# One decode block on Trainium2: a new order in TensorE's attention loop, and w_down's odd rows loaded another way

## The chip, the core and the metric

The kernel runs on one core of a Trainium2 chip. The metric is the device time of one execution in microseconds (us); its median over 15 runs is compared. A profile of one execution stands beside the times. The engines are called PE (TensorE's matmuls), PEld (TensorE's weight loads), DVE (VectorE), ACT (ScalarE), POOL (GpSimd) and SP (SyncE, which here only issues DMAs). L181 is line 181 of the kernel.

## What is computed

One token goes through an attention block with a cached K and V, and then through a gated feed-forward block. There are 32 heads of 128, 4096 cached positions, a model width of 640 and a feed-forward width of 1728. All inputs are bf16.

```python
def _A_ref(x, k_cache, v_cache, wq, wo):          # x: layernorm of the token
    q = (x @ wq).reshape(B, Sq, 32, 128).transpose(0, 2, 1, 3)
    scores = jnp.einsum("bhqd,bhkd->bhqk", q, k_cache) * (128 ** -0.5)
    o = jnp.einsum("bhqk,bhkd->bhqd", softmax(scores), v_cache)
    return o.transpose(0, 2, 1, 3).reshape(B, Sq, 4096) @ wo
def _B_ref(x, w_gate, w_up, w_down):
    return (gelu(x @ w_gate) * (x @ w_up)) @ w_down
x = A_x
h = x + _A_ref(layernorm(x), A_k_cache, A_v_cache, A_wq, A_wo)
h2 = h + _B_ref(layernorm(h), B_w_gate, B_w_up, B_w_down)
```

K and V are 32 MB each, so the kernel reads 84.2 MB for one token.

## The kernel before

**Stages.** The 32 heads are taken in eight stages (`NG`) of four heads. A stage's K is one DMA of 4 MB into one of two slots (`k_slot`), its V one DMA of 4 MB into the single `v_slot`; the last V goes into `k_slot[0]`. Partition 32h + p of a slot holds 128 consecutive positions of head h.

**Work of a stage G.** DVE multiplies K by the query in two halves, `mult(G, 0)` and `mult(G, 1)` (L368), into `prod`. TensorE adds up groups of the products with the identity matrix, `fold(e, 0)` and `fold(e, 1)`: 16 matmuls each into PSUM banks 0 to 3 (L349, and L181 for those that keep the weights). `probs(G)` then has DVE reduce the four banks to the scores (L374), ACT take the exponential (L375), and POOL multiply the result by the head mask `own` into `p_bd` (L377, called the mask multiply here). `pv` is 32 matmuls of `p_bd` with V into bank 5 (L356); ACT copies that bank out (L382), and `head_sum` (L362) picks the heads' parts.

**The order.** A small program builder (`Prog`) keeps a list of operations for each engine; each engine runs its list in order, and waits are written from the dependencies. TensorE's list has a hardware loop over k = 1 to 7, whose body is fold 0 of stage k, PV of stage k-1, fold 1 of stage k, head sum of stage k-1. The fold waits for its multiply and for the previous reduce. DVE's list has mult(1,0), the reduce of stage 0 and mult(1,1) at its start, and from then on both multiplies of a stage and then its reduce.

**SP's queue.** It issues W_q, K0, K1, V0, and then K2, V1, K3, V2 and so on to V7. A K load waits for the second multiply of the stage two before it; V(g) waits for PV(g-1). Behind them come W_o in two halves, w_down's odd rows, w_gate and w_up (both into `v_slot`, after PV 6), and the rest of w_down in four loads. w_down's 1728 rows are taken as three blocks of 512 (four rows to a partition) and 192 odd rows, the first of the matrix: 64 partitions with three rows each, in eight loads of eight partitions (L437 to L439), which wait for the last K multiply.

**The tail.** After PV 7 come the sums of the softmax, the output projection in two halves (L451), the residual and the second layernorm, the gate and up products (`glu`, L476, 75 matmuls each), the gelu on DVE and ACT (L483 to L491), and the down product (L494 to L506), whose first matmuls take the odd rows with 64 partitions. `pad_program` (L165) puts 200 instructions at the end of TensorE's program that are jumped over.

The constants come from POOL and DVE at the start: DVE clears bank 5 (L292) and builds `of_i` and `hs` from the identity matrices (L297, L298).

Of the kernel before, what the change touches and what calls it, by code (L numbers as in the profile page):

```python
# [5 lines left out]
FP32 = mybir.dt.float32  # L6
BF16 = mybir.dt.bfloat16
ALU = mybir.AluOpType
ACTF = mybir.ActivationFunctionType
AX = mybir.AxisListType  # L10

D = 640
# [8 lines left out]
NG = 8  # L21
# [140 lines left out]
                    inst.then_inc(lp.ev[ks[0], lp.body[n][0]].sem, 1)  # L162


def pad_program(nc, e, n):  # L165

    on = [e.engine]
    never = nc.alloc_registers("never", engines=on)
    nc.regs_mov(never, 0)
    nc.br_eq(nc.snap(never, min_val=0, max_val=1), 1, on_true="spare", on_false="done", engines=on)  # L170
    here = nc.cur_bb
    nc.switch_bb("spare")
    for i in range(n):
        e.nop(hint="n", nofuse=True)
    nc.br("done", engines=on)
    nc.switch_bb("done", parent=here)


def held(e, out, lhsT, rhs, start, stop):

    built = e.matmul(out, lhsT, rhs, start=start, stop=stop)  # L181
# [13 lines left out]
def bass_sequential_preLN__gqa_block_cached__glu_gated_geglu__decode_kernel(nc, A_x, A_k_cache, A_v_cache, A_wq, A_wo, B_x, B_w_gate, B_w_up, B_w_down, out):  # L195
    sb = lambda name, shape, dt: nc.alloc_sbuf_tensor(name, shape, dt)
# [5 lines left out]
    qb = sb("qb", [128, NG, DH], BF16)  # L202
    sc = sb("sc", [128, 128], FP32)
    pt = sb("pt", [128, 128], BF16)
    own = sb("own", [128, 4], BF16)
    p_bd = sb("p_bd", [128, 128, 4], BF16)
    RS = sb("RS", [128, NG], FP32)
# [8 lines left out]
    hlnT = sb("hlnT", [128, 5], BF16)  # L216
    po_sb = sb("po_sb", [128, 512], FP32)
    hs = sb("hs", [128, 4, 4], FP32)
# [3 lines left out]
    of_i = sb("of_i", [128, 32], BF16)  # L222
    g_t = sb("g_t", [128, 15], FP32)
# [6 lines left out]
    ones_f = sb("ones_f", [128, 128], FP32)  # L230
    mean_f = sb("mean_f", [128, 128], FP32)
    ones_b = sb("ones_b", [128, 128], BF16)
    id_f = sb("id_f", [128, 128], FP32)
    id_b = sb("id_b", [128, 128], BF16)
    eps_t = sb("eps_t", [128, 1], FP32)
# [3 lines left out]
    ps_f = psum[:, 0:2048]  # L239
    ps_q = [bank[0], bank[1]]  # L240
    ps_g, ps_u, ps_p = bank[0], bank[1], bank[2]
    ps_a = bank[4]
    ps_d = bank[3]
    ps_o = bank[5]
# [7 lines left out]
    P = Prog(nc)  # L252
    V = lambda fn, *d: P.op("vector", fn, *d)
    A = lambda fn, *d: P.op("scalar", fn, *d)
    T = lambda fn, *d: P.op("tensor", fn, *d)
    GP = lambda fn, *d: P.op("gpsimd", fn, *d)
# [9 lines left out]
    mults, pvs = {}, {}  # L266
# [10 lines left out]
    for kind, g in order[:3]:  # L277
# [8 lines left out]
    c_idb = GP(lambda e: e.affine_select(id_b[:, :], ones_b[:, :], pattern=[[1, 128]], compare_op=ALU.is_equal,  # L286
                                         fill=0.0, base=0, channel_multiplier=-1), c_onesb)
    c_ones = GP(lambda e: e.memset(ones_f[:, :], 1.0))
    c_idf = GP(lambda e: e.affine_select(id_f[:, :], ones_f[:, :], pattern=[[1, 128]], compare_op=ALU.is_equal,
                                         fill=0.0, base=0, channel_multiplier=-1), c_ones)  # L290

    c_po = V(lambda e: e.memset(ps_o, 0.0))  # L292
    own0 = GP(lambda e: e.affine_select(own[:, :], ones_b[:, 0:4], pattern=[[-32, 4]], compare_op=ALU.is_ge,
                                        fill=0.0, base=0, channel_multiplier=1), c_onesb)
    c_own = GP(lambda e: e.affine_select(own[:, :], own[:, :], pattern=[[32, 4]], compare_op=ALU.is_ge,
                                         fill=0.0, base=31, channel_multiplier=-1), own0)
    c_of = V(lambda e: e.tensor_reduce(of_i[:, :], id_b[:, :].rearrange("p (q i) -> p i q", q=4), axis=AX.X, op=ALU.max), c_idb)  # L297
    c_hs = V(lambda e: e.reduce_sum(hs[:, :, :], id_f[:, :].rearrange("p (t x r j) -> p x r j t", t=4, x=2, r=4)[:, 0, :, :, :],  # L298
                                    axis=AX.X), c_idf)


    def x_cols(e):
# [36 lines left out]

    reds, exps, blocks, evs, folds = {}, {}, {}, {}, {}  # L340
    VM = lambda fn, *d: P.op("vector", fn, *d, chan="m")
    VR = lambda fn, *d: P.op("vector", fn, *d, chan="r")
    AS = lambda fn, *d: P.op("scalar", fn, *d, chan="s")
    GS = lambda fn, *d: P.op("gpsimd", fn, *d, chan="s")

    def fold(e, i):
        for b in range(16):
            s, n = divmod(b, 8)
            mm = held if b else lambda e, *a, **k: e.matmul(*a, **k)  # L349
            r = mm(e, bank[2 * i + s], id_b[:, :], prod[:, i, 32 * s:32 * s + 32, 16 * n:16 * n + 16], start=(n == 0), stop=(n == 7))  # L350
        return r
# [14 lines left out]
    def mult(G, i):  # L366
        kt = view(k_slot[G % 2])
        mults[G, i] = VM(lambda e: e.tensor_tensor(  # L368
            out=prod[:, i, :, :], in0=kt[:, 64 * i:64 * i + 64, :],
            in1=qb[:, G, :].unsqueeze(1).to_broadcast([128, 64, DH]), op=ALU.mult),  # L370
            landed["K"][G], qa, qc, folds.get((G - 1, i)))

    def probs(G):
        reds[G] = VR(lambda e: e.reduce_sum(sc[:, :], ps_f.rearrange("p (g d) -> p g d", d=16), axis=AX.X), folds[G, 1])  # L374
        exps[G] = AS(lambda e: e.activation(pt[:, :], sc[:, :], ACTF.Exp, bias=zero_t[:, 0:1],  # L375
                                            scale=INV_SQRT_DH, accum_out=RS[:, G:G + 1]), reds[G], c_eps)
        blocks[G] = GS(lambda e: e.tensor_tensor(  # L377
            out=p_bd[:, :, :], in0=pt[:, :].unsqueeze(2).to_broadcast([128, 128, 4]),
            in1=own[:, :].unsqueeze(1).to_broadcast([128, 128, 4]), op=ALU.mult), exps[G], c_own)

    def evacuate(G):
        evs[G] = AS(lambda e: e.copy(po_sb[:, :], ps_o), pvs[G])  # L382

    def body_fold(i):
        return ("f%d" % i, lambda e, k: fold(e, i), lambda k: [mults[k, i], reds[k - 1]], True)

    for i in range(2):
        mult(0, i)
        folds[0, i] = T(lambda e, i=i: fold(e, i), mults[0, i], c_idb, qa, qc)
    T(None, c_hs, c_po)  # L390
    lp = P.loop("tensor", range(1, NG), [
        body_fold(0),
        ("pv", lambda e, k: pv(e, view(v_slot)), lambda k: [blocks[k - 1], landed["V"][k - 1]], True),
        body_fold(1),
        ("h", lambda e, k: head_sum(e, k * 4 - 4), lambda k: [evs[k - 1]], False)])
    for k in range(1, NG):
        for i in range(2):
# [1 line left out]
        pvs[k - 1] = lp.ev[k, "pv"]  # L399
    for kind, g in order[3:5]:  # L400
        load(kind, g)
    mult(1, 0)
    probs(0)
    mult(1, 1)
    for G in range(1, NG):
        if G > 1:
            mult(G, 0)
            mult(G, 1)
        for kind, g in order[3 + 2 * G:5 + 2 * G]:
            load(kind, g)  # L410
        evacuate(G - 1)
        probs(G)

    rt = GP(lambda e: e.tensor_tensor(out=RT[:, :, :], in0=RS[:, :].unsqueeze(2).to_broadcast([128, NG, 4]),
                                     in1=own[:, :].unsqueeze(1).to_broadcast([128, NG, 4]), op=ALU.mult), exps[NG - 1])
    pvs[NG - 1] = T(lambda e: pv(e, view(v_of(NG - 1))), blocks[NG - 1], landed["V"][NG - 1])
    T(lambda e: e.matmul(ps_z[:, 0:H], ones_f[:, :], RT[:, :, :].rearrange("p g j -> p (g j)"),
                         start=True, stop=True), rt, c_ones)
# [3 lines left out]
    at = V(lambda e: e.tensor_tensor(out=aT[:, :], in0=ps_a[:, 0:H], in1=RT[:, :, :].rearrange("p g j -> p (g j)"), op=ALU.mult), zr)  # L422
    as_ = V(lambda e: e.tensor_tensor(out=aS[:, :, :], in0=aT[:, :].unsqueeze(2).to_broadcast([128, H, 4]),
                                      in1=own[:, :].unsqueeze(1).to_broadcast([128, H, 4]), op=ALU.mult), at)
# [9 lines left out]
    wd_sb = k_slot[1][:, 0:15 * D].rearrange("p (m n) -> p m n", m=15)  # L434
    wd_v = B_w_down[192:1728, :].rearrange("(a p r) n -> p a r n", a=3, r=4)
    wd_d = wd_sb[:, 0:12, :].rearrange("p (a r) n -> p a r n", a=3)
    for o in (0, 1, 2, 3, 32, 33, 34, 35):  # L437
        d_wp = P.dma("sync", wd_sb[o:o + 29:4, 12:15, :],
                     B_w_down[0:192, :].rearrange("(p r) n -> p r n", r=3)[o:o + 29:4, :, :], mults[NG - 1, 1], chan="wp")  # L439
    d_wg = P.dma("sync", wg_sb, B_w_gate[:, :].rearrange("(p c) n -> p c n", c=5), pvs[NG - 2])  # L440
    d_wu = P.dma("sync", wu_sb, B_w_up[:, :].rearrange("(p c) n -> p c n", c=5))
    d_wd = [P.dma("sync", wd_d[:, a, lo:hi, :], wd_v[:, a, lo:hi, :])
# [28 lines left out]
    def glu(ps, w, *ws):  # L471
        def fn(e):
            for c in range(5):
                for m in range(15):
                    at, step = (192 + 512 * (m // 4) + m % 4, 4) if m < 12 else (m - 12, 3)
                    i = e.matmul(ps[:, m:m + 1], w[:, c, at:at + 127 * step + 1:step], hlnT[:, c:c + 1],  # L476
                                 start=(c == 0 and m == 0), stop=(c == 4), skip_group_check=True)
            return i
        return T(fn, *ws)
    ga = glu(ps_g, wg_sb, hl, d_wg)  # L480

    up = glu(ps_u, wu_sb, d_wu)
    g1 = V(lambda e: e.tensor_copy(g_t[:, :], ps_g[:, 0:15]), ga)  # L483
    g2 = V(lambda e: e.tensor_mul(t1[:, :], g_t[:, :], g_t[:, :]), g1)
    g3 = V(lambda e: e.scalar_tensor_tensor(out=t2[:, :], in0=t1[:, :], scalar=1.0 / GELU_C1, in1=g_t[:, :],
                                            op0=ALU.add, op1=ALU.mult), g2)
# [6 lines left out]
    def down(ms, qs=range(4)):  # L493
        def fn(e):  # L494
            for m in ms:
                for q in qs:
                    rows = 128 if m < 12 else 64
                    i = e.matmul(ps_d[32 * q:32 * q + 1, 0:160], hm[0:rows, m:m + 1],  # L498
                                 wd_sb[0:rows, m, 160 * q:160 * q + 160], start=False, stop=(m == 11))
            return i  # L500
        return fn
    T(down(range(12, 15)), g9, d_wp)
    T(down(range(4)), d_wd[0])
    T(down(range(4, 8)), d_wd[1])
    T(down(range(8, 11)), d_wd[2])
# [6 lines left out]
    P.op("sync", None, d_out)  # L512

    P.emit({"sync": 2})
    pad_program(nc, nc.tensor, 200)


# [26 lines left out]
```

## Time and profile before

| | us |
|---|---|
| median of 15 runs | 203.1 (202.2 to 204.7) |
| the profiled execution | 203.25 |
| its span, first to last instruction | 201.9 |
| busy: PE, DVE, POOL, ACT | 119.8, 98.8, 25.1, 12.6 |
| DMA: bytes moved, mean rate | 84.32 MB, 418 GB/s |

The profiled execution's time is 1.35 us longer than its span, which runs from the first to the last instruction of the program. The median is 0.15 us below that execution. In the profile's rows a group is given by line, engine, operation and tiles (written tile first, then what was read), with the number of instructions; in the timeline the columns are the start, the length, the group, and in brackets the idle time of the engine before it and what ended it. "Landing" is the moment at which a DMA's completion is counted; a load over all 128 partitions is spread over 16 DMA engines, and each of them counts its own completion.

### The profile page before, as it was taken

Reading aid. Unit: us, or ns where it says so; the run is one execution under the profiler, and the core shown is the slowest. Engines: PE = TensorE matmul, PEld = TensorE weight load, DVE = VectorE, ACT = ScalarE, POOL = GpSimd, SP = SyncE. Lnnn points to the kernel's source line nnn. Section 1 sums busy time; section 2 is a strip of 40 time slices with the busy share of each in tenths; the row PEclk is TensorE's granted clock in tenths of the full one; section 3 lists DMA queues with packets and bytes.
Section 4 is the critical chain, followed back from the end, with each engine's and each line's share of the span. In section 5 each row is a group of like instructions: output and inputs, shape, how many; then the busy total and the mean of one; then the engine's idle time right before and its main releaser. Section 6 shows DMA issues by size and latency. Waiting matters only on the chain.

```text
span 201.9 us, 1983 instructions
## 1 busy us (share of the span) xinstructions
PE 119.8 (59%) x1008; PEld 31.6 (16%) x748; DVE 98.8 (49%) x52; ACT 12.6 (6%) x33; POOL 25.1 (12%) x23
## 2 busy tenths in 40 slices
PE   0107029759908943990598069808940993976655
PEld 0101000001200120120012001200120012476543
DVE  2201196992299169627922791399149804020321
ACT  2101000000100100010001000100100010100101
POOL 3000000044062008002000200072010002000000
PEclk9999555967985995896579757975995599665555
DMA  9999999999999999999999999999999999999991
GB/s 357 414 404 461 428 422 422 422 467 441 419 422 415 415 428 467 448 422 415 415 422 474 441 428 415 415 422 474 428 435 422 415 422 441 410 427 434 423 387 58
DMA packets 3738, 84.32 MB, mean 418 GB/s; under 512 B 467, under 2 KB 597, under 8 KB 1045
## 3 DMA queue, kind: packets, MB, share of 16 engines
q1 hardware_dynamic: 3730, 84.23, 97.4%
q8 instruction: 5, 0.08, 0.2%
q10 hardware_dynamic: 2, 0.00, 0.0%
q14 instruction: 1, 0.00, 0.0%
HBM read 84.23 MB, written 0.00 MB: 417 GB/s over the span
## 4 chain that ended last, share of the span: by engine, by line
DMA 52%; PE 25%; DVE 19%; SPq 3%; issue 1%; DVEq 0%
DMA k_slot<-in_A_k_cache_dram 38%; PE psum L181 17%; DVE prod L368 15%; DMA v_slot<-in_B_w_up_dram 14%; PE psum L356 4%; DVE sc L374 3%; SPq L59 3%; PE psum L349 2%; PE psum L476 1%; PE psum L498 1%; DVE out_row L507 0%; DVE hm L491 0%; DVEq L114 0%
## 5 line engine op out<-in xcount | busy, mean ns | idle before, releaser
L368 DVE TENSOR_TENSOR prod<-k_slot,qb 128x8192 bf16<-128x8192 bf16 x16 | 73.2, 4608 | 12.1 <-DMA k_slot<-in_A_k_cache_dram 9.9
L181 PE MATMUL psum<-prod,id_b 128*128 128x512 bf16 x240 | 72.0, 467 | 0.0
L374 DVE TENSOR_REDUCE sc<-psum 128x128 f32<-128x2048 f32 x8 | 18.3, 2290 | 47.2 <-PE psum L181 47.2
L377 POOL TENSOR_TENSOR p_bd<-pt,own 128x512 bf16<-128x512 bf16 x8 | 23.1, 2892 | 145.5 <-ACT pt L375 145.5
L349 PE MATMUL psum<-prod,id_b 128*128 128x512 bf16 x16 | 7.9, 496 | 55.0 <-DVE prod L368 51.6
L356 PE MATMUL psum<-v_slot,p_bd 128*16 128x512 bf16 x224 | 13.3, 379 | 0.0
L349 PEld LDWEIGHTS psum<-prod,id_b 128*128 128x128 bf16 x16 | 1.6, 100 | 68.8 <-DVE prod L368 52.8
L356 PEld LDWEIGHTS psum<-v_slot,p_bd 128*16 128x16 bf16 x224 | 5.0, 89 | 45.3 <-DMA v_slot<-in_A_v_cache_dram 22.2
L362 PEld LDWEIGHTS psum<-hs,po_sb 128*128 128x128 f32 x64 | 8.3, 191 | 22.8 <-issue 22.1
L382 ACT COPY po_sb<-psum 128x512 f32<-128x512 f32 x7 | 4.1, 586 | 83.1 <-PE psum L356 83.1
L362 PE MATMUL psum<-hs,po_sb 128*128 128x4 f32 x64 | 7.7, 244 | 0.4 <-ACT po_sb L419 0.4
L451 PE MATMUL psum<-aP,arena 128*128 128x1 bf16 x160 | 6.7, 178 | 1.9 <-DMA arena<-in_A_wo_dram 1.8
L375 ACT ACTIVATE pt<-sc,zero_t 128x128 bf16<-128x128 f32 x8 | 3.2, 402 | 60.0 <-DVE sc L374 60.0
L331 PE MATMUL psum<-arena,xlnB 128*32 128x512 bf16 x20 | 2.8, 530 | 7.0 <-DMA arena<-in_A_wq_dram 7.0
L451 PEld LDWEIGHTS psum<-aP,arena 128*128 128x128 bf16 x160 | 6.6, 131 | 2.1 <-DMA arena<-in_A_wo_dram 1.9
L476 PE MATMUL psum<-hlnT,v_slot 128*128 128x1 bf16 x150 | 5.1, 171 | 2.5 <-DMA v_slot<-in_B_w_up_dram 2.5
L476 PEld LDWEIGHTS psum<-hlnT,v_slot 128*128 128x128 bf16 x150 | 5.0, 115 | 3.1 <-DMA v_slot<-in_B_w_up_dram 2.6
L356 PE MATMUL psum<-k_slot,p_bd 128*16 128x512 bf16 x32 | 3.4, 602 | 3.2 <-POOL p_bd L377 3.2
L336 DVE CAST qb<-psum 128x512 bf16<-128x512 f32 x1 | 0.7, 692 | 9.1 <-PE psum L181 9.1
L457 DVE COPY hT<-psum 128x5 f32<-128x5 f32 x1 | 0.2, 165 | 8.6 <-PE psum L451 8.6
L304 PE MATMUL psum<-one_bf,x_row 1*128 1x1 bf16 x5 | 0.4, 177 | 6.7 <-DMA x_row<-in_A_x_dram 6.7
L421 DVE RECIPROCAL RT<-psum 128x32 f32<-128x32 f32 x1 | 0.4, 357 | 6.9 <-PE psum L362 6.9
(63 smaller groups left out, 28.3 us busy)
## 6 DMA issues: line engine op xcount, KB each, us to landing
k_slot<-in_A_k_cache_dram SPq DMA_DIRECT2D x8, 4096.0 KB, 24.8
v_slot<-in_A_v_cache_dram SPq DMA_DIRECT2D x7, 4096.0 KB, 16.6
arena<-in_A_wq_dram SPq DMA_DIRECT2D x1, 5120.0 KB, 15.0
arena<-in_A_wo_dram SPq DMA_DIRECT2D x2, 2560.0 KB, 35.1
k_slot<-in_A_v_cache_dram SPq DMA_DIRECT2D x1, 4096.0 KB, 26.6
v_slot<-in_B_w_gate_dram SPq DMA_DIRECT2D x1, 2160.0 KB, 23.5
v_slot<-in_B_w_up_dram SPq DMA_DIRECT2D x1, 2160.0 KB, 28.2
k_slot<-in_B_w_down_dram SPq DMA_DIRECT2D x2, 640.0 KB, 30.1
```

Source lines behind the costliest of these rows:

```text
L59: ev = self.op(eng, lambda e: e.dma_start(out, in_), *deps, dma=True, chan=chan)
L181: built = e.matmul(out, lhsT, rhs, start=start, stop=stop)
L349: mm = held if b else lambda e, *a, **k: e.matmul(*a, **k)
L356: i = e.matmul(ps_o[a:a + 16, :], p_bd[:, 4 * b:4 * b + 4, :].rearrange("p g j -> p (g j)"), vt[:, 4 * b:4 * b + 4, :], start=(b < 4), sto ...
L362: i = e.matmul(ps_a[:, bass.ds(at, 4)], po_sb[:, 128 * r:128 * r + 128], hs[:, r, :], start=(r == 0), stop=(r == 3))
L368: mults[G, i] = VM(lambda e: e.tensor_tensor(out=prod[:, i, :, :], in0=kt[:, 64 * i:64 * i + 64, :], in1=qb[:, G, :].unsqueeze(1).to_broad ...
L374: reds[G] = VR(lambda e: e.reduce_sum(sc[:, :], ps_f.rearrange("p (g d) -> p g d", d=16), axis=AX.X), folds[G, 1])
L375: exps[G] = AS(lambda e: e.activation(pt[:, :], sc[:, :], ACTF.Exp, bias=zero_t[:, 0:1], scale=INV_SQRT_DH, accum_out=RS[:, G:G + 1]), red ...
L377: blocks[G] = GS(lambda e: e.tensor_tensor(out=p_bd[:, :, :], in0=pt[:, :].unsqueeze(2).to_broadcast([128, 128, 4]), in1=own[:, :].unsquee ...
L382: evs[G] = AS(lambda e: e.copy(po_sb[:, :], ps_o), pvs[G])
L451: r = e.matmul(ps_p[:, c:c + 1], wo_sb[:, i, c::5], aP[:, i:i + 1], start=False, stop=(i == 31), skip_group_check=True)
L476: i = e.matmul(ps[:, m:m + 1], w[:, c, at:at + 127 * step + 1:step], hlnT[:, c:c + 1], start=(c == 0 and m == 0), stop=(c == 4), skip_grou ...
```

## The change

The body of TensorE's loop becomes PV of stage k-1, fold 0, fold 1, head sum. The fold no longer waits for the reduce by itself, since PV, which now stands ahead of it, waits for what follows the reduce. Stage 0's reduce stands on DVE before both multiplies of stage 1. The mask multiply of stages 0 and 7 moves from POOL to DVE; for stage 0 a one-element memset on POOL passes the signal on.

w_down's 192 odd rows become one load of 128 rows, one to a partition, and eight loads of four partitions with two rows each into a new tile `wd_lo`, which POOL clears at the start. In `wd_lo` rows 0 to 15 and 32 to 47 hold data. The gate and up products take the matching columns with step 1 instead of 3, and the gate's copy becomes a multiply by `own_g`, which is zero in the partitions that hold no row. The down product takes 128 partitions once and 48 twice, instead of 64 three times.

Bank 5 is cleared by a matmul with zero weights (`none_b`) before the loop, and `hs` and `of_i` are made by four selects each on POOL. `pad_program` goes.

```diff
-def pad_program(nc, e, n):
...
-    c_po = V(lambda e: e.memset(ps_o, 0.0))
...
-    c_of = V(lambda e: e.tensor_reduce(of_i[:, :], ...
-    c_hs = V(lambda e: e.reduce_sum(hs[:, :, :], ...
+    c_hs = c_own
+    for t in range(4):
+        c_hs = GP(lambda e, at=at: e.affine_select(hs[at, :, :], ...
+    c_of = c_hs
+    for t in range(4):
+        c_of = GP(lambda e, at=at: e.affine_select(of_i[at, :], ...
+    c_none = GP(lambda e: e.memset(none_b[:, :], 0.0), c_of)
+    GP(lambda e: e.memset(own_g[:, 0:13], 1.0))
...
+    c_wd = GP(lambda e: e.memset(wd_lo[:, :, :], 0.0), c_gm)
...
+        on = V if G in (0, NG - 1) else GS
+        blocks[G] = on(lambda e: e.tensor_tensor(
             out=p_bd[:, :, :], in0=pt[:, :].unsqueeze(2).to_broadcast([128, 128, 4]),
             in1=own[:, :].unsqueeze(1).to_broadcast([128, 128, 4]), op=ALU.mult), exps[G], c_own)
+        if G == 0:
+            blocks[G] = GS(lambda e: e.memset(spare[:, :], 0.0), blocks[G])
...
-        return ("f%d" % i, lambda e, k: fold(e, i), lambda k: [mults[k, i], reds[k - 1]], True)
+        return ("f%d" % i, lambda e, k: fold(e, i), lambda k: [mults[k, i]], True)
...
-    T(None, c_hs, c_po)
+    T(lambda e: e.matmul(ps_o, none_b[:, :], qb[:, 0:4, :].rearrange("p g d -> p (g d)"), start=True, stop=True), c_none)
+    T(None, c_hs)
     lp = P.loop("tensor", range(1, NG), [
-        body_fold(0),
         ("pv", lambda e, k: pv(e, view(v_slot)), lambda k: [blocks[k - 1], landed["V"][k - 1]], True),
-        body_fold(1),
+        body_fold(0), body_fold(1),
         ("h", lambda e, k: head_sum(e, k * 4 - 4), lambda k: [evs[k - 1]], False)])
...
-    mult(1, 0)
     probs(0)
-    mult(1, 1)
     for G in range(1, NG):
-        if G > 1:
-            mult(G, 0)
-            mult(G, 1)
+        mult(G, 0)
+        mult(G, 1)
...
+    d_w1 = P.dma("sync", wd_sb[:, 12, :], B_w_down[64:192, :], mults[NG - 1, 1])
     for o in (0, 1, 2, 3, 32, 33, 34, 35):
-        d_wp = P.dma("sync", wd_sb[o:o + 29:4, 12:15, :],
-                     B_w_down[0:192, :].rearrange("(p r) n -> p r n", r=3)[o:o + 29:4, :, :], mults[NG - 1, 1], chan="wp")
+        lo = o - o % 32
+        d_wp = P.dma("sync", wd_lo[o:o + 13:4, :, :],
+                     B_w_down[lo:lo + 32, :].rearrange("(r i q) n -> q i r n", q=4, r=2)[o - lo, :, :, :], c_wd, chan="wp")
...
-    g1 = V(lambda e: e.tensor_copy(g_t[:, :], ps_g[:, 0:15]), ga)
+    g1 = V(lambda e: e.tensor_tensor(out=g_t[:, :], in0=ps_g[:, 0:15], in1=own_g[:, :], op=ALU.mult), ga, c_gm)
...
-                    rows = 128 if m < 12 else 64
+                    rows, wd = (128, wd_sb[:, m]) if m < 13 else (48, wd_lo[:, m - 13])
...
-    T(down(range(12, 15)), g9, d_wp)
+    T(down([12]), g9, d_w1)
+    T(down([13, 14]), d_wp)
...
-    pad_program(nc, nc.tensor, 200)
```

## The prediction

> **What bounds the kernel now.** I read the page's slices first, because they say whether any engine matters at all.
>
> ```profile
> span 201.9 us, 1983 instructions
> ...
> DMA  9999999999999999999999999999999999999991
> ...
> q1 hardware_dynamic: 3730, 84.23, 97.4%
> q8 instruction: 5, 0.08, 0.2%
> ```
>
> The 16 DMA engines are full from the first slice to the last but one. The change moves the same bytes, so it can only act on holes in that stream, on how evenly its tail falls on the 16 engines, and on work behind the last landings. The chain that ended last, in order of time, shows the tail:
>
> ```profile
> 166.57 28.21 DMA v_slot<-in_B_w_up_dram
> 194.78 0.05 issue
> 194.83 2.58 PE psum L476 x75
> ...
> 197.73 2.35 PE psum L498 x51
> 200.08 0.30 DVE out_row L507
> ```
>
> w_up lands at 194.78, its product takes 2.58, the down product 2.35. In the trace's landing records the last w_down load completes on its sixteenth engine at 199.70, and the last four matmuls start at 199.74: two chains end within 0.4 us of each other. The same records show an uneven stream. From 64 us on, two engines complete every K and V load about 1.0 us after the third-last (V6: 160.46, then 161.46, 161.52). A 16 KB packet of the instruction queue (52.66, 183.72, 193.14, each 1.0 us) sits on one DMA engine, and the data packet behind it is 0.35 to 0.55 us longer: some 1.5 us for each. The last load's completions are 196.91 to 198.40 on fourteen engines, then 199.47 and 199.70.
>
> Last, the timeline of the last attention stage, where the new order acts:
>
> ```profile
> 156.70 5.57 PE L181 MATMUL psum<-prod,id_b 128*128 128x512 bf16 x15
> 162.21 1.90 PE L356 MATMUL psum<-v_slot,p_bd 128*16 128x512 bf16 x32
> 164.04 0.39 PE L349 MATMUL psum<-prod,id_b 128*128 128x512 bf16 x1
> 164.27 3.40 PE L181 MATMUL psum<-prod,id_b 128*128 128x512 bf16 x15
> 167.71 2.29 DVE L374 TENSOR_REDUCE sc<-psum 128x128 f32<-128x2048 f32 x1 [7.13 <-PE psum L181]
> 170.03 0.40 ACT L375 ACTIVATE pt<-sc,zero_t 128x128 bf16<-128x128 f32 x1 [5.28 <-DVE sc L374]
> 170.60 1.04 POOL L377 TENSOR_TENSOR p_bd<-pt,own 128x512 bf16<-128x512 bf16 x1 [18.90 <-ACT pt L375]
> 171.69 3.39 PE L356 MATMUL psum<-k_slot,p_bd 128*16 128x512 bf16 x32 [3.24 <-POOL p_bd L377]
> ```
>
> Fold 0 runs from 156.30 to 162.21 while V6 is still landing (161.52). PV, fold 1, reduce, exp, mask and the last PV follow.
>
> **PV first in the loop.** V(k-1) lands one load after K(k), so fold 0 of every stage, which needed only K(k), now stands on TensorE behind a PV that waits for V(k-1) and for the mask; behind fold 0 wait fold 1, DVE's reduce, ACT's copy and SP's next V load. The work after that landing becomes PV 1.83 (162.21 to 164.04) and two folds at full clock, 3.63 each (164.04 to 167.67): 9.09. To this comes the cold start. Granted clock is 0.5 when a stage begins, and fold 0 shows its price: 5.30 to 6.48 us over the seven stages, against 3.63 for fold 1, so 1.67 to 2.85, mean 2.25. Today that is paid before V lands; now it is paid after. Fold 1 then ends at 161.57 + 9.09 + 2.25 = 172.9 instead of 167.67: 5.2 later (4.7 to 5.8).
>
> [...]
>
> Most stages have cover. DVE has to reduce (2.29) and then multiply the next K (two of 4.8, beside POOL) after fold 1, which ends 23.4 us after V(k-1) landed; V(k) lands after 19.4, and its PV and fold 0 cover the other 4.0. V(k+1)'s load is issued when PV(k) ends, 1.9 us after V(k) landed today and about 3.4 then; K(k+2) still has over 6 us to run. So the stream keeps its next load and the steady stages cost nothing; without that cover each would cost the excess.
>
> In the last stage the shift goes on. The reduce and exp keep their durations. The mask goes to DVE, which is idle there. VectorE multiplies with the same broadcast took 0.29 for 128 elements and 0.82 for 640 f32; POOL took 1.04. I take 0.67 for 512 (0.165 for five elements, plus four times 0.127), so 0.4 saved (0.2 to 0.75). The last PV took 3.32 because the clock had fallen at 171.33, 2.9 us after the loop's last matmul; then it starts 2.8 us after it. Half a warm PV is worth 0.75 (0 to 1.5). PV ends 5.2 - 0.4 - 0.75 = 4.05 later, and so does the first half of the output projection: 185.7 instead of 181.66. The second half waited for W_o until 183.49, so it starts 2.25 late, and the gate product ends at 192.36 + 2.25 = 194.6. w_up lands at 194.78. The cover is used up but for 0.2, and the bounds give -1.2 to +1.3 around it: on average I charge 0.25.
>
> **The 192 odd rows of w_down.** 64 packets of 3840 B at 149 ns (9.5 us of engine time) become 192 of 1280 B at 55 ns (10.6): 0.07 per engine if spread evenly. It is not even. Chaining packets end to start, today's 64 sit on eight engines, eight packets each (1.2 us), and the two late engines carry none. The new 128-partition load gives every engine eight packets: 0.44, also the late ones. The 64 rows left, 3.5 us of engine time, add between 0.22 (all engines) and 0.88 (four engines). On the late engine that ends last I take 0.45 (0.44 to 1.32): last landing 200.15. On the eight, the fast engine hit at 183.72, which sets w_up's landing, goes from 1.2 to between 0.44 and 1.32: -0.8 to +0.1.
>
> [...]
>
> SP's queue: the first small load waits for the last K multiply, 160.58 now and about 165.5 then. Nine issues at 0.66 and the six large ones (2.8) are behind it, done by 174.3; the DMA engines reach them at 181.4. Cover 7 us, cost zero.
>
> **Edits with one answer.** The eight selects and the memsets on POOL run at the start: the present set ends at 3.0, and even a 2.1 us memset for wd_lo ends by 8.5; TensorE needs them at 39. The DVE work they replace lies before x lands at 6.7. The zeroing matmul (0.39) stands at 39.0, when TensorE is idle until 42.4. In stage 0 the reduce and the mask stand on DVE before both multiplies of K1; the mask waits some 0.6 for ACT's exp, and those multiplies wait behind it: the second ends at 51.5 instead of 46.7. K3's load waits for it, but V1's, issued before, is 10 us long. The mask's signal passes over POOL (a memset of 0.1) at 42.8; V0 lands at 44.15. The gate mask costs a copy's 0.174, under the wait for w_up. Down's changed row counts bring one more change of height; the pause at such a change is 0.26 (197.97 to 198.23), covered by the wait for w_down.
>
> **The pad.** TensorE's never-run code goes. The fifth instruction packet (201.11 to 202.05) outlives the span; its absence saves 0 to 0.14. If the others then fall on other DMA engines, that costs up to 1.5 or saves as much. I take 0, the value for packets that fall where they fell.
>
> **Sum.** Last landing +0.45, gate product +0.25: +0.7 on the profiled execution's 203.25 gives 203.95. The median stands 0.15 below that execution, so 203.8. A measurement of this kernel tells about 0.3% (0.6 us) from no change.
>
> **Rivals.** *The hole at 52.5 closes (faster).* V1 is issued at 50.90, when PV 0 ends, and K2's engines run dry at 52.48 to 53.40. The two late engines start V1 at 53.75 and 53.84 with packets of 1.68 instead of 1.21; that is where they become late. PV first issues V1 at about 47.6 (V0 lands at 44.15, a cold PV takes 3.4). If both catch up, the end moves from 199.70 to the third-last engine's 198.40 plus 0.45: -0.85; 203.1 - 0.85 = 202.3. For it: the times fit. Against: one of the two also carried the instruction packet at 52.66, which stays.
>
> *Nothing shows.* One engine catches up and its 0.45 is returned, the gate product stays hidden: 203.1, within 0.6.
>
> *The loop becomes the bound (much slower).* PV(k) needs the mask of stage k: 9.09 + 2.25 + reduce 2.3 + exp and hand-over 0.65 + POOL 4.6 (its time beside DVE multiplies, against 1.04 alone) = 18.9, against 19.4 between V landings. At the cold price's upper end, 2.85, and POOL's longest, 5.1, it is 20.0. If that held, six stages would each lag 0.6, 3.6 in all, less the cover of 0.2: 206.5. It decides from 19.4 on. Against: the mean lies 0.5 below.
>
> **Chances.** Forecast 0.5 (its own range 203.4, the landing's 0.44 less the pad's 0.14, to 204.4, the 1.3 of the gate product or of four engines), hole closes 0.24, nothing 0.16, loop bound 0.1. A tenth of the forecast lies within 0.6 of 203.1: faster 0.24, same 0.16 + 0.05 = 0.21, slower 0.45 + 0.1 = 0.55. Range 202.2 to 205.2: it leaves out most of the loop case and the far end of the hole case.
>
> **What would show it.** PV starts each stage within 0.1 of V's landing, fold 0 after it; the last PV at about 176.5; the gate product ending near 194.6; POOL's masks at 4.6 in every middle stage; "under 2 KB" up by 192 packets and 16 completions. Wrong if the last PV moves by less than 3 us, if V's last completions lose their 1.0 us lag (the hole was the cause), or if PV starts wait for POOL.

## The result

| | before | after |
|---|---|---|
| median of all runs, us | 203.22 (202.2 to 204.7) | 204.78 (203.87 to 205.0) |
| profiled execution, span | 203.25, 201.9 | 204.83, 203.5 |
| V6's last completion | 161.52 | 161.91 |
| last PV starts | 171.69 | 176.49 |
| gate product ends | 192.36 | 195.30 |
| w_up's last completion | 194.78 | 194.57 |
| up product ends | 197.40 | 198.88 |
| w_down's last completion | 199.70 | 199.26 |
| copies of the output start | 200.07 | 201.60 |

The changed kernel takes 1.0072 times as long, 95% interval 1.0050 to 1.0093: about 1.5 us slower. The last loads did not land later; TensorE got later. The page's first and DMA lines after:

```profile
span 203.5 us, 1995 instructions
...
DMA  9999999999999999999999999999999999999980
...
q1 hardware_dynamic: 3842, 84.23, 96.8%
q8 instruction: 4, 0.07, 0.1%
```

The stream is as full as before, except in the last two slices, where before it was full up to the last. The chain of waits that ended last, in order of time (start, length, what), shows what ends the execution now:

```profile
192.08 0.71 PE psum L465 x8
192.80 4.72 PE psum L486 x144
197.52 1.05 issue
198.57 0.33 PE psum L486 x6
...
198.99 0.18 DVE hm L501
199.17 0.04 issue
199.21 2.40 PE psum L508 x39
201.62 0.30 DVE out_row L518
```

Before, this chain held a DMA piece that ended with w_up at 194.78, and TensorE's timeline before has the wait for it:

```profile
189.80 2.56 PE L476 MATMUL psum<-hlnT,v_slot 128*128 128x1 bf16 x75
...
194.83 2.57 PE L476 MATMUL psum<-hlnT,v_slot 128*128 128x1 bf16 x75 [2.47 <-DMA v_slot<-in_B_w_up_dram]
```

After, no load stands in the chain behind 161.91. The gate product and the up product (L486, 75 matmuls each) run back to back, since w_up is there before the gate product ends; and after 144 of the 150 matmuls TensorE stops for 1.05 us, for nothing that the profile names ("issue"). The last stage in the timeline:

```profile
161.96 3.59 PE L359 MATMUL psum<-v_slot,p_bd 128*16 128x512 bf16 x32 [8.22 <-DMA v_slot<-in_A_v_cache_dram]
...
165.48 0.61 PE L352 MATMUL psum<-prod,id_b 128*128 128x512 bf16 x1
...
165.88 3.52 PE L167 MATMUL psum<-prod,id_b 128*128 128x512 bf16 x15
...
169.45 3.40 PE L167 MATMUL psum<-prod,id_b 128*128 128x512 bf16 x15
...
172.89 2.29 DVE L377 TENSOR_REDUCE sc<-psum 128x128 f32<-128x2048 f32 x1 [8.11 <-PE psum L167]
...
175.74 0.69 DVE L381 TENSOR_TENSOR p_bd<-pt,own 128x512 bf16<-128x512 bf16 x1 [0.56 <-ACT pt L378]
...
176.49 3.50 PE L359 MATMUL psum<-k_slot,p_bd 128*16 128x512 bf16 x32 [2.85 <-DVE p_bd L381]
```

PV starts 0.05 after V6's last completion and takes 3.5 us, not 1.9, because the granted clock is 0.5 there, from 155.87 to 166.11 (before, it was 1.0 from 161.09 to 171.33; work at 0.5 is called cold below, work at 1.0 warm). The folds follow at 165.48, and the reduce and the last PV come 5.2 and 4.8 later than before.

Put together from the two profiles: the gate product ends 2.94 later; 2.47 of that was the time for which TensorE used to wait for w_up; 0.47 is left, and the stop adds 1.05. That is 1.52, and the output copies start 1.53 later. The profiled execution is 1.58 longer.

### The profile page after: what moved, and what is told of

Read it like the earlier page. It is cut to its first block, busy times and chain, and to the rows that moved or that the text cites. A ratio compares the mean times of both kernels' runs of the same rounds, so it can differ in the third digit from the quotient of the medians.

```text
span 203.5 us, 1995 instructions
## 1 busy us (share of the span) xinstructions
PE 118.0 (58%) x1009; PEld 33.9 (17%) x749; DVE 100.7 (49%) x51; ACT 12.6 (6%) x33; POOL 33.8 (17%) x36
## 4 chain that ended last, share of the span: by engine, by line
DMA 68%; PE 26%; DVE 3%; issue 1%; ACT 1%; SPq 0%; DVEq 0%
DMA v_slot<-in_A_v_cache_dram 68%; PE psum L359 14%; PE psum L456 3%; PE psum L167 3%; PE psum L486 2%; PE psum L508 1%; DVE sc L377 1%; PE psum L365 1%; PE psum L352 0%; DVE hX L469 0%; PE psum L465 0%; DVE p_bd L381 0%; DVE out_row L518 0%; PE psum L315 0%; ACT po_sb L422 0%
## 5 line engine op out<-in xcount | busy, mean ns | idle before, releaser
L371 DVE TENSOR_TENSOR prod<-k_slot,qb 128x8192 bf16<-128x8192 bf16 x16 | 75.1, 4733 | 4.6 <-DMA k_slot<-in_A_k_cache_dram 4.6
L167 PE MATMUL psum<-prod,id_b 128*128 128x512 bf16 x240 | 58.8, 401 | 0.0
L359 PE MATMUL psum<-v_slot,p_bd 128*16 128x512 bf16 x224 | 24.9, 625 | 51.9 <-DMA v_slot<-in_A_v_cache_dram 51.9
L381 POOL TENSOR_TENSOR p_bd<-pt,own 128x512 bf16<-128x512 bf16 x6 | 27.7, 4622 | 90.8 <-ACT pt L378 90.8
L359 PEld LDWEIGHTS psum<-v_slot,p_bd 128*16 128x16 bf16 x224 | 7.0, 124 | 64.6 <-DMA v_slot<-in_A_v_cache_dram 52.9
L352 PE MATMUL psum<-prod,id_b 128*128 128x512 bf16 x16 | 7.5, 466 | 9.8 <-DVE prod L371 9.8
L335 PE MATMUL psum<-arena,xlnB 128*32 128x512 bf16 x20 | 3.3, 626 | 6.9 <-DMA arena<-in_A_wq_dram 6.9
L486 PE MATMUL psum<-hlnT,v_slot 128*128 128x1 bf16 x150 | 5.1, 171 | 1.0 <-issue 1.0
L486 PEld LDWEIGHTS psum<-hlnT,v_slot 128*128 128x128 bf16 x150 | 5.0, 115 | 1.6 <-issue 1.1
```

The costliest lines, as they stand in the source:

```text
L335: mm = held if hf else lambda e, *a, **k: e.matmul(*a, **k)
L359: i = e.matmul(ps_o[a:a + 16, :], p_bd[:, 4 * b:4 * b + 4, :].rearrange("p g j -> p (g j)"), vt[:, 4 * b:4 * b + 4, :], start=(b < 4), sto ...
L371: mults[G, i] = VM(lambda e: e.tensor_tensor(out=prod[:, i, :, :], in0=kt[:, 64 * i:64 * i + 64, :], in1=qb[:, G, :].unsqueeze(1).to_broad ...
L381: blocks[G] = on(lambda e: e.tensor_tensor(out=p_bd[:, :, :], in0=pt[:, :].unsqueeze(2).to_broadcast([128, 128, 4]), in1=own[:, :].unsquee ...
L486: i = e.matmul(ps[:, m:m + 1], ws, hlnT[:, c:c + 1], start=(c == 0 and m == 0), stop=(c == 4), skip_group_check=True)
```

## Theories

**L (late).** The new order puts TensorE's cold work after V's landing, so its last layer is later by more than the cover, and with the cover (the wait for w_up) the place is gone where TensorE's next piece of code could arrive unnoticed. The stop is that arrival. The trace has 16 KB packets of the instruction queue, one of them at 195.95 in the profile after, 1.03 long; TensorE goes on 1.59 after its end. **Rivals:** the missing `pad_program` moved the code packets or the stop (P); the new w_down loads, the constants or the masks cost something themselves (D); the stop only wanders, so that no placing of the code is rid of it (Q); the two late DMA engines come from the hole in the stream at 52.5 (H). These letters stand in the expectations too.

## Experiments

**1. The pad put back.**

```diff
 # after, and:
+def pad_program(nc, e, n): ...
     P.emit({"sync": 2})
+    pad_program(nc, nc.tensor, 200)
```

> The changed kernel with the 200 jumped-over instructions put back at the end of TensorE's program. Theory L (late code): in the changed kernel the gate and the up product run back to back, and TensorE stops 1.05 us near the end of the up product because the code behind it is fetched only while the gate product runs; the pad lies behind all of that, so the stop stays and the time is the changed kernel's, 204.8 within 0.4. Rival P (the pad): without the pad the fetches come too late, so with it the stop goes and the time falls by about 1.0, to 203.8.

Measured: 204.65, ratio to before 1.0086 (1.0052 to 1.0120). The chain:

```profile
191.90 4.72 PE psum L500 x144
196.63 1.21 issue
197.84 0.33 PE psum L500 x6
```

The stop stays at the same matmul; its packet ran from 195.23 to 196.26, and TensorE went on 1.58 later. There are five instruction packets again, the last outside the path. P falls.

**2. The pad taken from the kernel before.**

```diff
 # before, and:
-    pad_program(nc, nc.tensor, 200)
```

> The kernel before without the pad, nothing else changed. Theory L: TensorE waits 2.5 us for w_up between the two products, the code arrives in that time, so no stop: 203.2 within 0.4, four instruction packets instead of five. Rival P: a stop of about 1 us appears in the up product, 204.2.

Measured: 203.25, ratio 1.0000 (0.9977 to 1.0023). No stop shows; TensorE waits for w_up until 195.17. The pad is worth nothing in either kernel.

**3. The loop's order alone.**

```diff
 # before, and:
     lp = P.loop("tensor", range(1, NG), [
-        body_fold(0),
         ("pv", ...),
-        body_fold(1),
+        body_fold(0), body_fold(1),
```

> The kernel before with PV ahead of fold 0 in the loop and nothing else. Theory L: the last PV starts about 5 us later (176.5 to 177), the gate product ends near 195.3, the up product follows without a wait for w_up and stops 1.0 us for its code: 204.4 to 204.9, nearly the whole change. Rival P: no stop, only the 0.35 of the up product's later end: 203.6. Rival D (w_down's loads cost the time): under 203.6 as well.

Measured: 205.27, ratio 1.0110 (1.0076 to 1.0144), more than expected.

```profile
193.25 4.79 PE psum L475 x145
198.03 0.97 issue
199.01 0.33 PE psum L475 x5
```

The stop is there with the order alone, none of the other edits being in. The half us above the expectation isn't a late V: V1 was issued at 51.51 (after: 48.10) and its first completion came at 63.16 (after: 62.68), but V6's last came at 161.56 (after: 161.91), and the last PV started at 176.02, 0.47 before that of the profile after. It lies behind that PV:

```profile
180.31 1.88 PE psum L362 x8
```

The granted clock fell to 0.5 at 174.88 and stayed there; after, it fell at 176.35 and was 1.0 again from 179.76 to 183.18, and the same head sum took 1.07 in its chain. So the output projection starts at 183.67 (after: 183.22) and the gate product ends at 195.76 (after: 195.30).

**4. The new w_down loads alone,** with their columns in the gate and up products, `own_g`, and the new down product.

```diff
 # before, and:
+    d_w1 = P.dma("sync", wd_sb[:, 12, :], B_w_down[64:192, :], mults[NG - 1, 1])
     for o in (0, 1, 2, 3, 32, 33, 34, 35):
-        d_wp = ... wd_sb[o:o + 29:4, 12:15, :] ...
+        d_wp = ... wd_lo[o:o + 13:4, :, :] ...
```

> The kernel before with the new loads of w_down's odd rows alone (128 rows one to a partition, eight loads of four partitions, the tile cleared on POOL, gate mask, 128 and 48 rows in the down product). Theory L: the attention order and the wait for w_up are unchanged; the last landing moves by the 0.45 that the 128-partition load adds to the late engine: 203.2 to 203.8. Rival D: this part carries the time, 204.2 to 204.8.

Measured: 202.95, ratio 1.0004 (0.9982 to 1.0025). w_up completes at 194.83 (before 194.78), the last w_down load at 199.51 (before 199.70). These loads cost nothing here.

**5. The code moved.** 64 no-operations that TensorE runs once, early, while it waits for K0 anyway.

```diff
 # after, and behind the q projection:
+    T(lambda e: [e.nop(hint="n", nofuse=True) for _ in range(64)][-1])
```

> The changed kernel with 64 empty instructions that TensorE runs after the query projection (it is idle there), so that all later code lies 64 instructions further on. Theory L (late code): code comes in pieces of 16 KB (256 instructions); the piece whose edge lies six matmuls before the end of the up product now begins 64 instructions earlier in the program's work, and the edge before it lies in the output projection, some 7 us ahead instead of 4.2; the stop of 1.05 us goes and the time falls to 203.6 to 204.0. Rival S: the stop belongs to that place in the up product (its data or its semaphore); it stays and the time is 204.8 as before.

Measured: 203.52, ratio 1.0026 (1.0002 to 1.0050).

```profile
185.97 3.36 PE psum L457 x84
189.33 0.14 issue
189.47 0.37 PE psum L457 x5
...
192.85 4.91 PE psum L487 x150
...
198.08 2.40 PE psum L509 x60
```

The 150 matmuls now run without a stop. This is the experiment that tells the stop's cause: the work and its order are the same, and only the instructions' places in the program have moved. Against 1.0072 it gives back 0.46%, 0.9 us, where the stop was 1.05. The remaining 0.14 at 189.33 falls five matmuls before the projection's end.

**6. Fold 0 first again on TensorE, all else as after.**

```diff
 # after, and:
+        body_fold(0),
         ("pv", ...),
-        body_fold(0), body_fold(1),
+        body_fold(1),
 # and the folds wait for the reduce of the stage before by its own count
```

> The changed kernel with fold 0 ahead of PV again (and the fold's own wait for the reduce), all else as changed. Theory L: the last PV goes back to about 171.5, the gate product ends near 192.5, TensorE waits for w_up again and there is no stop: 202.9 to 203.5, the kernel before. Rival: the constants, the masks, stage 0's order or the loads carry some of the time, 203.8 or more.

Measured: 206.26, ratio 1.0178 (1.0140 to 1.0215). The expectation was missed. The page's rows by slice (5.1 us each) say where:

```profile
DMA  9999999999699999999999999999999999999991
GB/s 369 393 445 430 411 411 475 443 417 411 218 437 475 417 411 424 456 449 408 417 430 469 430 411 417 437 469 424 411 417 443 475 411 399 437 403 430 430 396 61
```

In the eleventh slice, 51 to 56 us, the stream has a hole: 218 GB/s. On DVE stage 0's reduce and mask stand ahead of both multiplies of K1, so with fold 0 first PV 0 starts only at 51.51, V1 is issued at 53.46, and by then K2's engines have run dry. V1 completes at 65.0 to 65.6 on all engines, the first 2.3 us later than before and the last 1.2; w_up lands at 196.96. So the orders on TensorE and on DVE must be undone together, which is experiment 10.

**7. TensorE kept busy.** 28 matmuls of the identity with the query, into a bank that nothing reads, at the head of each turn of the loop.

```diff
 # after, and:
     lp = P.loop("tensor", range(1, NG), [
+        ("w", lambda e, k: warm(e), lambda k: [], False),
```

> The changed kernel with 28 idle matmuls (identity times the query, into bank 7, which nothing reads) at the head of each loop iteration, which keep TensorE busy while it waits for V. Theory L with the cold start as its first cause: PV, the folds and perhaps the last PV run at full clock, fold 1 of the last stage ends about 1.8 earlier and the last PV takes 1.8 instead of 3.5; the gate product then ends 2 to 3 us earlier, near 192.5, w_up is waited for, the code comes in that time: 203.0 to 203.7. Rival C (the clock isn't what shifts the stage): last PV at 176 as before, 204.8.

Measured: 203.98, ratio 1.0029 (1.0001 to 1.0057), in two groups, five runs at 202.63 to 202.78 and seven at 203.86 to 204.50. The profiled execution is of the upper group. There the expectation was missed: the clock was 0.5 from 162.81 to 166.22 all the same, PV took 2.65, the last PV started at 175.99, and the gate product ended at 194.45, after w_up's last completion at 194.42, so that nothing covered the stop.

```profile
194.46 1.93 PE psum L493 x55
196.39 1.40 issue
197.79 0.81 PE psum L493 x20
```

The stop now comes after 130 of the 150 matmuls, not after 144. A matmul of this kind is two instructions, a weight load and the matmul (L486 has 150 of each in the profile after), so it has moved by 28 instructions: 28 matmuls and one weight load had been put in ahead of it. The stop is tied to a place in the program. What sets the two groups apart isn't shown, as only one of them has a profile.

**8. PV first in stage 1 alone,** the loop from stage 2 on in the old order.

```diff
 # before, and:
-        blocks[G] = GS(lambda e: e.tensor_tensor(
+        blocks[G] = (V if G == 0 else GS)(lambda e: e.tensor_tensor(
+    # pv(0), fold(0), fold(1), head_sum(0) of stage 1 ahead of the loop
-    lp = P.loop("tensor", range(1, NG), [
+    lp = P.loop("tensor", range(2, NG), [
```

> The kernel before with PV ahead of fold 0 in stage 1 alone (that iteration written out ahead of the loop) and stage 0's mask multiply on DVE. Theory H (the hole at 52.5): V1's load is issued near 48 instead of 50.9, the DMA engines find their next packets, and the completions of V1 and all later loads lose the late engine's lag; the last stage keeps its order. The last landing falls by 0.3 to 0.9: 202.3 to 202.9. Rival: the lag belongs to the instruction packet, not to the hole: 203.1.

Measured: 203.77, ratio 1.0043 (1.0015 to 1.0072). V1 was issued at 48.29, so the hole at 52.5 is closed; yet there are two late engines all the same, at 64.14 and 64.41 in V1, and at 54.42 and 54.70 already in K2. One completion was 0.97 behind the fourteenth in V0 (44.72), before any hole, and between V0 and K2 lies an instruction packet at 49.06. So H falls: the hole isn't needed for late engines. It may have added to them in the kernel before, where the last but one is 0.24 behind the fourteenth in K2 and 1.02 in V1; in this kernel K2 and V1 have the same spacing. What made this kernel slower is w_up's landing at 195.50 (before: 194.78). Its packets of code ran at 181.17 and 188.29, where before there were others at 183.72 and 193.14; that they fell on an engine that was late already would explain it, and wasn't tried by itself.

**9. Kept busy, and the code moved:** 5 and 7 together.

> The kernel after with 28 idle matmuls at the head of each turn of TensorE's loop and with 64 no-operations that TensorE executes once after the q projection, so that the edges of its 16 KB code pieces fall elsewhere. Theory L (TensorE's last layer is later by the cold multiplies after V lands and by the stop for code): the last PV starts at about 176.0, the gate product ends at about 194.5, no stop inside the up product, which ends at about 197.0; the down product ends between 199.5 and 200.0 and the time is 202.6 to 203.3, not slower than before. Rival Q (the stop only moves, to wherever TensorE runs without a pause): a stop of 1.0 to 1.4 us in the projection or the gate product, and 203.8 to 204.6.

Measured: 203.24, ratio 1.0015 (0.9994 to 1.0035).

```profile
161.78 1.90 PE L359 MATMUL psum<-v_slot,p_bd 128*16 128x512 bf16 x32 [0.84 <-DMA v_slot<-in_A_v_cache_dram]
...
174.33 2.46 PE L359 MATMUL psum<-k_slot,p_bd 128*16 128x512 bf16 x32 [2.85 <-DVE p_bd L381]
...
186.97 0.92 PE L464 MATMUL psum<-aP,arena 128*128 128x1 bf16 x20 [0.38 <-issue]
...
190.84 2.57 PE L494 MATMUL psum<-hlnT,v_slot 128*128 128x1 bf16 x75
...
194.42 2.58 PE L494 MATMUL psum<-hlnT,v_slot 128*128 128x1 bf16 x75 [1.01 <-DMA v_slot<-in_B_w_up_dram]
```

PV runs warm as soon as V6 has landed (1.90), the last PV starts at 174.33, 1.7 earlier than expected and 2.16 earlier than after (PV is 1.69 shorter, fold 0 0.29, and V6 landed 0.18 earlier), and the up product waits for w_up again, 1.01 us. Q falls: the code's edge shows as a stop of 0.38 in the projection, and costs nothing there, since w_up is waited for afterwards.

**10. The whole old order, all else as after.**

```diff
 # after, and:
+        body_fold(0),
         ("pv", ...),
-        body_fold(0), body_fold(1),
+        body_fold(1),
...
+    mult(1, 0)
     probs(0)
+    mult(1, 1)
 # and stage 0's mask on POOL
```

> The kernel after with the old order alone: on TensorE fold 0 ahead of PV, on VectorE the stage 1 multiply of half 0 ahead of stage 0's probabilities, and stage 0's mask multiply on GpSimd; the w_down loads, the constants, the last mask on VectorE and the missing pad stay as in the kernel after. Theory L: the order is the whole loss, so the last PV starts near 171.7 + 0.1, the up product waits for w_up, no stop for code shows, and the time is 202.8 to 203.5. Rival D (the new w_down loads, the constants or the mask on VectorE cost something of their own beside the order): 203.9 to 204.8.

Measured: 203.02, ratio 1.0015 (0.9988 to 1.0041). The last PV starts at 172.05.

```profile
167.32 27.02 DMA v_slot<-in_B_w_up_dram
194.33 0.05 issue
194.38 2.58 PE psum L488 x75
...
197.29 2.40 PE psum L510 x34
```

The order is undone and the loss is gone, with the w_down loads, the constants, the mask of the last stage on DVE and the missing pad all in. D falls.

**11. Experiment 3 with the code moved:** 64 no-operations as in 5.

> The kernel before with PV ahead of fold 0 in TensorE's loop as the only change of the order, and with 64 no-operations that TensorE executes once after the q projection. Theory L: against the same order without them (205.27, a stop of 0.97) the stop is gone and the time is 204.0 to 204.5; what is left over the kernel before is the hole of stage 1's loads and the late cold PV. Rival Q (the stop moves to another place of TensorE's last layer): 205.0 to 205.5.

Measured: 204.24, ratio 1.0058 (1.0030 to 1.0086); experiment 3 had 205.27.

```profile
193.44 4.93 PE psum L476 x150
```

The stop is gone. The gate product ends at 195.95 here and at 195.76 there, the up product at 198.36 and 199.32; so the 1.03 us between the two kernels is in the main the stop of 0.97. The same edit has taken the same term out of two kernels. What is left over the kernel before starts with V6, whose last completion came at 162.48 (before: 161.52), so that the last PV started at 177.37. V1 had three late completions here (64.43 to 65.34), before two; whether the hole made the third, as the expectation has it, isn't shown.

No kernel here beats the one before. Those that come down to it (4, 9 and 10) wait for w_up, which completes between 194.33 and 194.83 in all of them.

## Why the prediction was near, and where its steps failed

**The shift on TensorE: right, by two errors that cancel.** Fold 1 was put at 172.9 and ended at 172.85, the last PV at 176.5 and started at 176.49. But PV could start at 161.96, behind V6's landing at 161.91, not at 161.57, and the cold start cost 1.82 (PV 3.52 instead of 1.83, fold 0 3.76 instead of 3.63), not 2.25. Over the seven stages, from PV's start to fold 0's end against 5.46 warm, the price is 1.36 to 2.60, mean 2.03.

**The last PV: a term of 0.75 that did not come.** The prediction let the clock fall 2.9 us after the loop's last matmul, so that half of this PV would run warm. The granted clock in two windows of the profile after (start and end, length, busy time of each engine; the third value from the end is PE's granted clock):

```profile
166.11:176.35 10.24, 7.53 (x39) 1.15 (x9) 2.90 (x2) 0.57 (x3) 0.56 (x1) 1.00 0.98 418
176.35:179.76 3.41, 3.27 (x32) 0.98 (x32) 0.09 (x1) 0.00 (x0) 0.18 (x1) 0.50 0.97 414
```

The clock fell at 176.35, 0.14 before this PV began. PV started 4.80 later and, nearly all of it cold, ended 4.91 later instead of 4.05; the gate product ended 2.94 later instead of 2.25: 195.30 against the 194.6 forecast. That turns a gate product that just fits under w_up's landing into one that ends 0.7 after it. (The bounds put around this place, -1.2 to +1.3, are not the sum of those named for its terms, which is -1.8 to +1.4; 0.7 lies in both.)

**The missing term: the stop, 1.05.** The prediction read the instruction packets only as load on DMA engines, and asked for the pad on which engine they fall. It didn't ask who waits for what they bring. TensorE does. Before, 2.47 us of waiting for w_up covered it; the change used that cover up for the shift, and the same cover was needed twice. This is two thirds of the loss, and experiments 5 and 11 each show it by taking it away.

**The w_down loads: 0.45 too much.** The last landing was to move to 200.15; it came at 199.26, and TensorE, at its last matmuls later than that, doesn't wait for it. Alone (experiment 4) the loads moved it by -0.19. Which engine carried what in the end differs from profile to profile with the code packets, so the sign of these tenths stays open; that the loads cost no time does not. Packets of 1280 B rose by 192 as forecast, but completions fell by 16 instead of rising: eight loads that each counted on 8 engines now count on 4 (64 completions less 32), and the new full load adds 16. So each load of four partitions counted on four engines; which four isn't shown.

**The pauses and small edits: right in their cost.** DVE's mask took 0.69 (forecast 0.67). The pause of 0.26 where the down product changes height is still there, no longer covered, but the wait for the last w_down load that covered it is gone as well: the down product takes 2.40, before 2.35. SP issued the odd rows' loads from 164.8 and ended its issues at 179.7, later than the 174.3 forecast; the engines finished W_o, which is ahead of them, at 182 to 184. The clearing of `wd_lo`, put at 2.1 at most, took 1.16 and ended at 7.4.

**The rivals.** The hole closed as the first rival said (V1 issued at 48.10), but two late engines were there, 0.6 and 1.5 behind: closing it did not rid the stream of them, as experiment 8 shows too. The loop did not become the bound, by little. POOL's mask:

```profile
L381 POOL TENSOR_TENSOR p_bd<-pt,own 128x512 bf16<-128x512 bf16 x6 | 27.7, 4622 | 90.8 <-ACT pt L378 90.8
```

It took 4.62 in each of six stages. The closest was the one that began at 79.41 and ended at 84.03; V2's last completion came at 84.18. So every PV did start within 0.05 of V's landing, and the cover there was 0.15.

**The sum.** Forecast +0.7: 0.25 for the gate product and 0.45 for the landing. It was +1.58: 0.47, nothing, 1.05, and 0.06 behind the output. The sign was right, and so was the shift that uses up TensorE's cover. But 0.45 of the 0.7 forecast did not come, and 1.05 of the 1.58 measured was not forecast. The measured 204.78 lies above the forecast's own 203.4 to 204.4; that it lies inside the whole range, to 205.2, is luck, since the upper end was there for the loop case, which did not happen.

## What to carry to other kernels

A wait that looks idle may cover more than one thing, as the 2.47 us of waiting for w_up did here: before spending it, list everything that falls into it, the arrival of code included. Where a long unrolled stretch (here 128 matmuls with their weight loads, 4.2 us) has no wait in it and the DMA engines are full, look at its instruction packets and test with executed no-operations (here 64), put where the engine waits anyway, whether the edge of a code piece can lie elsewhere. Putting work behind a landing moves its cold start there too, so cost it cold (the PV behind V6 took 3.52 us instead of 1.83).

## What the runs showed of the hardware

**Code comes in pieces, counted here at 254 to 256 instructions, and its arrival can be the bound.** Each packet of the instruction queue is 16384 B. A pause in experiment 5 lies at 189.33, five matmuls before the projection's end; 64 instructions move the edge of the profile after by 32 matmuls, from 144 to 112 of the 150 (counted, since no stop shows there), and between the two lie 5 + 2 + 8 + 112 = 127 matmuls with their weight loads, 254 instructions. Experiments 7 and 9, counted in the same way, give 20 + 2 + 8 + 98 = 128 matmuls, 256 instructions. So in the profile after, the edge before the stop is near the 16th gate matmul, at about 193.25. The packet started 2.7 us later, took 1.03, and TensorE went on 1.59 after it (1.37 to 1.58 in experiments 1, 3, 5, 7 and 9): 5.3 in all, against 4.2 of work between two edges. Experiment 9 has 29 more instructions ahead of that place than experiment 5, which puts the earlier edge 19.5 matmuls ahead of the projection's end, and the pause there has 20 matmuls behind it. And the stop grows roughly with the packet's delay after the earlier edge: 2.69 and 2.72 us with stops of 1.05 and 0.97 (after, experiment 3), 2.86 with 1.21 (1), 3.34 with 1.40 (7). That the packet started late because the DMA engines were full is likely, but was not tried by itself.

**The clock changed on a grid.** The changes of the granted clock in the profile after (155.87, 166.11, 176.35, 179.76, 183.18) lie 10.24, 10.24, 3.41 and 3.42 apart, multiples of 3.41; before, all changes from 17.73 to 178.16 lie 3.41, 6.83, 10.24 or 13.65 apart. The PV behind V6 took 3.52 in the profile after, 1.90 in experiment 9, and 2.65 in experiment 7, which has the same 28 matmuls as 9, but a clock of 0.5 from 162.81 to 166.22. So keeping TensorE busy ahead of a PV did not by itself settle its clock; that the place of the work on the grid settles the rest is the author's estimate, and was not tried.

**Behind an instruction packet a DMA engine was late, and it stayed late for 84 and 110 us.** Experiment 6 shows it by itself, since its packet came late, at 93.14. In V2 and K3 the last of the sixteen completions comes 0.19 after the fourteenth; in K4, behind the packet, 1.73 after it (96.30 and 94.57), and in the first half of W_o, 84 us on, still 1.75. In the profile after, the last two of V0's completions come 0.02 and 0.63 after the fourteenth (43.79), so one engine was late already; those of K2, behind the packet at 49.42, come 0.62 and 1.52 after it (53.52), and for V6, 110 us later, it is 0.62 and 1.54. So in these two stretches nothing caught up. Across the hole of experiment 6 it did: the last completion is 0.76 behind the fourteenth in V0 and 0.19 in V1, with the slice of 218 GB/s between the two.
